# The first token group of a Mamba2 scan with a GELU network behind it: `a` in rows, B and C turned in blocks, another order of loads, y in the bank area

## The chip, the cores and the metric

The kernel runs on one core of one Trainium2 chip. The metric is the time of one execution on the device in microseconds; several executions are timed and the median is given. One further execution is taken with the hardware profiler, and every profile line below is from that one. PE is the matrix engine (PEld its weight loads), DVE the vector engine, ACT the scalar engine, POOL the general one, and SP the engine that here only issues DMAs.

## What is computed

A selective state space scan (Mamba2 SSD) over 4 batches of 8 heads, 768 positions, head dimension 32 and state dimension 16, and then a two-layer network with the quick GELU over the 3072 tokens. Cut to what matters:

```python
log_a = np.log(np.clip(a, 1e-06, 1.0))
for c in range(nc):                       # chunks along the sequence
    cum = np.cumsum(la, axis=-1)
    L = np.exp(cum[:, :, :, None] - cum[:, :, None, :]) * causal
    CB = np.einsum('bhin,bhjn->bhij', Cc, Bc)
    y_intra = np.einsum('bhij,bhjd->bhid', CB * L, xc)
    y_inter = np.einsum('bhin,bhnd->bhid', Cc, state) * decay_to_i[:, :, :, None]
    y[:, :, sl] = y_intra + y_inter
    state = decay_full[:, :, None, None] * state + np.sum(Bx, axis=2)
x = y.transpose(0, 2, 1, 3).reshape(3072, 256)
h = x @ w_in                              # 256 x 2048, given as float64
g = h * (1.0 / (1.0 + np.exp(-1.702 * h)))
out = (g @ w_out).astype(np.float32)      # 2048 x 256, given as float64
```

The two weight matrices come in as 64-bit floats and are made into 32-bit ones on the chip.

## The kernel before

**Tiling.** The 3072 tokens are six groups of 512 (`TG`). A group is two *pairs*, numbered p = 0 to 11; a pair is two blocks `k` of 128 positions, and each block has two chunks (`SIDES`) of 64. Groups 1 to 5 go through the same steps as group 0, but for groups 1 and later much of the work is laid between the matrix products of the group before it. Group 0 has nothing to hide behind. This document is about group 0 and the hand-over to what follows.

**A pair's scan.** `differ` puts differences of the cumulated logs of `a` into PSUM (after `mask` has put in the causal mask), `decay_exp` makes the decay matrix `L` of them. `turn_only` turns B and C with four transposes on PE and copies the results out of PSUM: `BT`, the per-head-masked `CT`, and plain C. `score` multiplies them into `cb`, `weigh` multiplies `L` by `cb` on DVE. `ends` scales B by the decay to the chunk's end, `gain` multiplies by x into the states' increments, `keep` (`part_of`, then `add_up`) turns these into states on DVE. `since_exp` and `since_start` scale C by the decay since the sequence's start. `finish` then makes y from two parts, `inter` (states) and `intra` (`L` and x), and ACT copies y to `yT`, or, for pair 0, to `early_y`.

**The first group's own form.** Rows of `a` come four times into 32 partitions each, 512 columns wide (`az0`), and are clipped, logged and scanned (L310 to L318) into `cum`. Pair 0's y lies in two PSUM banks, so `inter` is split into two halves around `intra`, tied by a POOL memset of `spare` (L738). Later pairs (`apart`) have y in the four-bank area `psa`.

**The network.** w_in comes in six pieces and w_out in four (`PIECES`; four small ones of 512 columns for hidden blocks 0 to 7, the rest with 1024). Piece i goes through `fields` (two DVE operations on the high words), `clamp` (two on ACT), `rounded` and `join` (one and two on DVE); `narrow(i)` is `rounded(i)`, `fields(i + 1)`, `join(i)`. `join` of some pieces also issues the load of a later one (`NEXT`). `half(j, t)` makes two hidden blocks for one pair (t = 0 for pair 0), `hidden(0, f)` one block for the whole group, and `project_all` the outputs. Before, blocks 0 to 3 are made in halves: `half(0, 0)` and `half(1, 0)` for pair 0, the second with four filling matmul instructions of ones, then `finish((1,))`, then `half(0, 1)` and `half(1, 1)`.

**What sets the order.** Every engine runs its instructions in the order in which the program text issues them (`in_order` adds that order as dependencies). PSUM has four banks in a ring (`bank`, tag `ff`) and one four-bank area (`area`, tag `cb`). The order of group 0 is written out by hand from L1043 to L1098, and what is laid into the hidden and project loops is listed by `at(...)` from L1106 on. All loads go through SP's queue in program order, but for two of `a`'s and C of pair 0 on ACT's:

```python
    rows_a(az0, (nc.sync, nc.scalar))
    ...
    load(0, nc.scalar)
    table(AF.Ln)
    fetch(0)
    load(1)
    for i in range(1, 4):
        fetch(i)
    rows_a(az, (nc.sync,))
```

Of the kernel before, what the change touches and what calls it, by code (L numbers as in the profile page):

```python
# [16 lines left out]
P = 128  # L17
# [18 lines left out]
def kernel(  # L36
# [71 lines left out]
    az0 = ssd.tile([P, CG, P], FP32, tag="CT", name="az0")  # L108
    cum = ffn.tile([P, 4 * TG // 2], FP32, tag="mg", name="cum", bufs=3)[:, :CG * P].rearrange(
        "p (c s) -> p c s", c=CG)  # L110
# [6 lines left out]
    def load_blocks(p):  # L117

        g, n = divmod(p, PG)
        b, c = divmod(2 * p, NC)  # L120
        for name, src in (("B", B), ("C", C)):
            if n == 0:
                blocks[name, g] = raw.tile([P, 2, PG * P], FP32, tag="z", name=f"z{name}{g}", bufs=2)
            for r in range(R):
                nc.sync.dma_start(
                    out=blocks[name, g][32 * r:32 * r + 32, :, n * P:(n + 1) * P],
                    in_=src[b, 2 * r:2 * r + 2, c * P:(c + 2) * P].rearrange(
                        "h (i f) n -> i h (f n)", i=32))

    def load(p, queue=nc.sync):  # L130
        rb[p] = raw.tile([P, 2, NH, N], FP32, tag="b", name=f"b{p}", bufs=3)
        if p < 2 * PG:
            rc[p] = raw.tile([P, 2, NH, N], FP32, tag="c", name=f"c{p}", bufs=3)
        else:
            load_blocks(p)
        rx[p] = raw.tile([P, 2, NH, D], FP32, tag="x", name=f"x{p}", bufs=3)
        for dst, src in ((rb, B), (rc, C), (rx, x)):
            for k in range(2 if p in dst else 0):
                b, c = divmod(2 * p + k, NC)
                sl = slice(c * P, (c + 1) * P)  # L140
                (queue if dst is rc else nc.sync).dma_start(out=dst[p][:, k], in_=src[b, :, sl, :].rearrange("h s d -> s h d"))  # L141
# [116 lines left out]
    rows_a(az0, (nc.sync, nc.scalar))  # L258
    early = const.tile([P, 1], FP32, name="early")
    spare = const.tile([P, 1], FP32, name="spare")  # L260
# [6 lines left out]
    load(0, nc.scalar)  # L267
    table(AF.Ln)
    fetch(0)
    load(1)  # L270
    for i in range(1, 4):
# [34 lines left out]
    carry = ssd.tile([P, NC, P], FP32, tag="first", name="carry", bufs=1)  # L306
    nc.vector.memset(carry[:, :CG], 1.0)
    nc.vector.memset(carry[:, :CG].rearrange(by_chunk, s=2)[:, :, :, 0], 0.0)

    nc.vector.tensor_scalar(out=az0, in0=az0, scalar1=1e-6, scalar2=1.0, op0=ALU.max,  # L310
                            op1=ALU.min)
    for k in range(2):
        nc.scalar.activation(cum[:, 2 * k:2 * k + 2], az0[:, 2 * k:2 * k + 2], AF.Ln)
    table(AF.Exp)
    for k in range(2):
        t = cum[:, 2 * k:2 * k + 2].rearrange("p c s -> p (c s)")

        nc.vector.tensor_tensor_scan(  # L318
            out=t, data0=carry[:, 2 * k:2 * k + 2].rearrange("p c s -> p (c s)"), data1=t,
            initial=0.0, op0=ALU.mult, op1=ALU.add)  # L320
# [12 lines left out]
    def pick_a(p):  # L333
# [4 lines left out]
        for q in range(Q):  # L338
# [3 lines left out]
    whose = const.tile([32, NH, N], FP32, name="whose")  # L342
    nc.gpsimd.memset(whose, 1.0)
    nc.gpsimd.affine_select(out=whose, in_=whose, pattern=[[-1, NH], [0, N]],
                            compare_op=ALU.is_equal, fill=0.0, base=0, channel_multiplier=1)


# [8 lines left out]
    idents = const.tile([P, 2 * NH, H], FP32, name="idents")  # L356
# [41 lines left out]
    def keep_busy(n):  # L398

        t = bank("busy")  # L400
        for i in range(n):
            nc.tensor.matmul(out=t, lhsT=ones, rhs=ones.unsqueeze(1).to_broadcast([P, 4, P]),
# [46 lines left out]
    def fan_rows(t, c0, c1):  # L449

        o = bank(f"rows{c0}")[:, :(c1 - c0) * P]
        nc.tensor.matmul(out=o, lhsT=whose.rearrange("p h n -> p (h n)"),
# [878 lines left out]
```

## Time and profile before

| what | value |
|---|---|
| median of three runs | 358.86 us (357.01, 358.86, 360.74) |
| the profiled execution | 359.47 us |
| its span | 357.4 us |
| granted TensorE clock, mean | 0.995 |
| busy PE / DVE / ACT / POOL | 349.4 / 251.6 / 148.7 / 10.5 us |
| first projection product (o) starts | 53.91 us |

The span is the time between the first and the last instruction of the program in the profile. Busy time is summed over each engine's instructions; a line such as `L212` is a line of the kernel's text. A timeline row has the start, the length, engine, line, operation, the tile written and the tiles read, the number of instructions merged into the row, and in brackets how long the engine was idle before it and what ended that. Rows of merged instructions may contain short gaps.

### The profile page before, as it was taken

What the parts mean: (1) busy time and instruction counts of PE and PEld (TensorE: products, weight loads), DVE (VectorE), ACT (ScalarE), POOL (GpSimd) and SP (SyncE); (2) the same over time, 40 slices, a digit from 0 to 9 for tenths busy, and PEclk for the clock granted to TensorE, in tenths of its full rate; (3) what the DMA queues carried; (4) which work ended last, traced back from release to release, by engine and by line L of the source; (5) the groups of instructions that cost most, each with busy time, mean ns of one, the idle gap of its engine ahead of it and who ended that gap; (6) DMA issues with size and microseconds to landing.
All of it is one profiled execution on the core that took longest, in us unless ns stands there. A gap on an engine that the chain in (4) does not pass through costs nothing.

```text
span 357.4 us, 9060 instructions
## 1 busy us (share of the span) xinstructions
PE 349.4 (98%) x3884; PEld 301.0 (84%) x3884; DVE 251.6 (70%) x480; ACT 148.7 (42%) x334; POOL 10.5 (3%) x36
## 2 busy tenths in 40 slices
PE   8979999999999999999999999999999999999996
PEld 3756448887679999889999889999989999989996
DVE  5777997999887999687588366588374344365363
ACT  5648837212353421753423454333454331453320
POOL 4200000100000100000000000000000000000000
PEclk9989999999999999999999999999999999999999
DMA  9897688316672000565006044000010000010001
GB/s 155 198 350 162 176 194 193 64 17 193 110 144 61 0 2 2 81 186 105 2 7 124 5 106 91 0 2 2 1 62 2 2 1 2 0 59 2 0 2 59
DMA packets 74527, 26.10 MB, mean 73 GB/s; under 512 B 60536, under 2 KB 67960, under 8 KB 74488
## 3 DMA queue, kind: packets, MB, share of 16 engines
q1 hardware_dynamic: 71896, 25.08, 30.0%
q10 hardware_dynamic: 2592, 0.46, 0.7%
q8 instruction: 30, 0.49, 0.6%
q14 instruction: 9, 0.07, 0.1%
HBM read 22.28 MB, written 3.24 MB: 71 GB/s over the span
## 4 chain that ended last, share of the span: by engine, by line
PE 89%; DVE 4%; SPq 2%; DMA 2%; ACT 1%; issue 1%
PE acc L956 35%; PE X L850 18%; PE Y L860 13%; PE o L892 8%; PE h L774 6%; PE y L728 2%; SPq L141 2%; PE y L705 2%; PE cb L597 2%; DMA bits<-in_moe_w_in_dram 1%; PE A L628 1%; PE h L792 1%; DVE p L206 1%; DMA az<-in_a_dram 1%; DVE w_in L212 1%
## 5 line engine op out<-in xcount | busy, mean ns | idle before, releaser
L956 PEld LDWEIGHTS acc<-mw,mg 128*128 128x128 f32 x480 | 67.1, 191 | 4.0
L956 PE MATMUL acc<-mw,mg 128*128 128x128 f32 x480 | 68.9, 275 | 0.0
L855 ACT ACTIVATE ac<-X 128x256 f32<-128x256 f32 x76 | 29.1, 382 | 83.5 <-PE X L850 83.0
L975 DVE TENSOR_TENSOR gT<-Y,ac 128x512 f32<-128x512 f32 x38 | 26.2, 690 | 41.3 <-PE Y L860 36.3
L827 ACT ACTIVATE gT<-gT 128x512 f32<-128x512 f32 (+1 forms) x76 | 39.3, 519 | 32.3 <-DVE gT L975 31.8
L956 PEld LDWEIGHTS acc<-w_out,gT 128*128 128x128 f32 x320 | 44.1, 191 | 2.6
L956 PE MATMUL acc<-w_out,gT 128*128 128x128 f32 x320 | 45.3, 275 | 0.0
L850 PE MATMUL X<-my,mi 128*128 128x256 f32 x152 | 45.2, 380 | 0.0
L975 DVE TENSOR_TENSOR gT<-Y,b 128x256 f32<-128x256 f32 x38 | 15.9, 420 | 35.0 <-PE Y L860 35.0
L892 PE MATMUL o<-w_out,gT 128*128 128x256 f32 x128 | 28.6, 381 | 0.0
L774 PE MATMUL h<-yT,w_in 128*128 128x512 f32 x64 | 28.3, 595 | 0.2 <-DVE w_in L212 0.2
L818 DVE TENSOR_TENSOR mg<-gT 128x512 f32<-128x512 f32 x40 | 27.2, 681 | 0.0
L892 PEld LDWEIGHTS o<-w_out,gT 128*128 128x128 f32 x128 | 23.9, 190 | 3.5 <-DVE w_out L212 0.2
L850 PEld LDWEIGHTS X<-my,mi 128*128 128x128 f32 x152 | 24.7, 191 | 1.3
L956 PEld LDWEIGHTS acc<-mw,gT 128*128 128x128 f32 x160 | 23.1, 191 | 1.8
L956 PE MATMUL acc<-mw,gT 128*128 128x128 f32 x160 | 24.3, 276 | 0.0
L774 PEld LDWEIGHTS h<-yT,w_in 128*128 128x128 f32 x64 | 11.9, 190 | 14.6 <-issue 12.7
L956 PE MATMUL acc<-w_out,mg 128*128 128x128 f32 x160 | 24.0, 275 | 0.0
L956 PEld LDWEIGHTS acc<-w_out,mg 128*128 128x128 f32 x160 | 22.8, 191 | 1.2
L855 ACT ACTIVATE b<-X 128x256 f32<-128x256 f32 x38 | 14.6, 383 | 21.4 <-PE X L850 20.9
L850 PE MATMUL X<-yT,w_in 128*128 128x256 f32 x76 | 23.3, 391 | 0.0
L860 PE MATMUL Y<-yT,mi 128*128 128x256 f32 x76 | 22.8, 381 | 0.3 <-DVE gT L975 0.3
(143 smaller groups left out, 510.2 us busy)
## 6 DMA issues: line engine op xcount, KB each, us to landing
a<-scratch SPq DMA_DIRECT2D x18, 256.0 KB
bits<-in_moe_w_out_dram SPq DMA_DIRECT2D x4, 1024.0 KB
x<-in_x_dram SPq DMA_DIRECT2D x24, 128.0 KB
out_dram<-c SPq DMA_DIRECT2D x9, 256.0 KB
bits<-in_moe_w_in_dram SPq DMA_DIRECT2D x4, 512.0 KB
bits<-in_moe_w_in_dram SPq DMA_DIRECT2D x2, 1024.0 KB
b<-in_B_dram SPq DMA_DIRECT2D x24, 64.0 KB
af<-in_a_dram SPq DMA_DIRECT2D x3, 384.0 KB
```

The lines of the kernel that those rows point to most:

```text
L141: (queue if dst is rc else nc.sync).dma_start(out=dst[p][:, k], in_=src[b, :, sl, :].rearrange("h s d -> s h d"))
L597: nc.tensor.matmul(out=s["cb"][side, r, k].rearrange("p (q i) -> p q i", q=Q), lhsT=BT[rows, k, side], rhs=CT[rows, k, :, side], start=Tru ...
L705: nc.tensor.matmul(out=y[i][to:to + Q * D, t, 2 * n + k], lhsT=old[rows], rhs=st[p]["CsT"][rows, k, SIDES[i]], start=begin(i, t, range(Q * ...
L774: nc.tensor.matmul(out=h, lhsT=w_in[:, k, f * P:(f + 1) * P], rhs=yT[g][:, k], start=(k == 0), stop=(k == NK - 1))
L818: nc.vector.tensor_tensor(out=t[:, 0:2], in0=B[:, :, 1], in1=B[:, 0], op=ALU.subtract)
L827: nc.scalar.activation(o, i, AF.Silu, scale=GELU_SCALE)
L850: nc.tensor.matmul(out=s["X"], lhsT=lhsT, rhs=rhs, start=i == "1", stop=i == "4", skip_group_check=True)
L855: nc.scalar.activation(copy, s["X"], AF.Copy)
L860: nc.tensor.matmul(out=o, lhsT=lhsT, rhs=rhs, start=s.pop("new", False), stop=i != "5", skip_group_check=True)
L892: nc.tensor.matmul(out=o[k // 2][:, k % 2], lhsT=gT[g, f // 2][:, f % 2, k * P:(k + 1) * P], rhs=w_out[:, f], start=(f == 0 and k % 2 == 0 ...
L956: nc.tensor.matmul(out=o[k] if type(o) is list else o[:, cols], lhsT=h[:, cols], rhs=w, start=(j == 0 and (i, k) in begins), stop=(j == NF ...
L975: nc.vector.tensor_tensor(out=o, in0=v, in1=w, op=ALU.add)
```

## The change

It concerns group 0, and the places of group 1's work that are listed beside it.

- `az0` and `cum` hold pair 0's and pair 1's 256 positions of batch 0 in different rows, 256 columns instead of 512; one log, one scan. `differ` reads row sets 0 and 2 (`ROW`), and `whose` gets four row sets. `since_exp` is done per pair.
- B and C of pair 0 are also loaded in 512-byte runs (`load_blocks`, now two DMAs for each of B and C instead of four, with `queues`), and turned by DVE (`turn_first`) instead of PE; `mask_first` makes `CT`. Pair 0's B is still loaded in the other form for `ends`.
- The loads come in another order: blocks, piece 0, b0, x0, then C and B of pair 1, piece 1, x of pair 1, pieces 2 and 3.
- Pair 0's decay matrix is made by one exponential over the area; pair 1's masks and differences come directly after pair 0's.
- `finish` has y in the area for all pairs; for pairs 0 and 1 `intra` goes ahead of `inter`. The `spare` memset and the ties are gone.
- Only blocks 0 and 1 are made in halves, with pair 1's score and decay between the two blocks of `half(0, 0)`. The filling matmuls in `half` are gone, and those of `keep_busy` are four times as many of a quarter of the width. The explicit load of the Silu table is gone.
- `narrow`, `clamp` and group 1's steps have other places in the loops of group 0.

```diff
-    az0 = ssd.tile([P, CG, P], FP32, tag="CT", name="az0")
+    az0 = const.tile([P, 2, P], FP32, name="az0")
+    cum = const.tile([P, 2, P], FP32, name="cum")
...
+            for h in range(2):
+                queue.dma_start(
+                    out=blocks[name, g][:, h, n * P:(n + 1) * P],
+                    in_=src[b, h::2, c * P:(c + 2) * P].rearrange("r (i f) n -> r i (f n)", i=32))
...
-    rows_a(az0, (nc.sync, nc.scalar))
+    for r in range(R):
+        (nc.sync, nc.scalar)[r % 2].dma_start(
+            out=az0[32 * r:32 * r + 32].rearrange("p k s -> p (k s)"),
+            in_=a[:2, :, :TG].rearrange("b h (c s) -> c (b h) s", c=PG))
...
-    load(0, nc.scalar)
+    load_blocks(0, (nc.scalar, nc.sync))
     table(AF.Ln)
     fetch(0)
-    load(1)
-    for i in range(1, 4):
+    load(0, "b")
+    load(0, "x")
+    load(1, "cb")
+    fetch(1)
+    load(1, "x")
+    for i in range(2, 4):
         fetch(i)
...
+    def turn_first(name):
+        t = ssd.tile([P, TG], FP32, tag=f"{name}t", name=f"{name}t0", bufs=1)[:, :2 * P]
+        nc.vector.transpose(
+            out=t.rearrange("p (i f) -> p f i", i=32),
+            in_=blocks.pop((name, 0))[:, :, :P].rearrange("p h (f n) -> p f h n", n=N))
...
+    def mask_first():
+        s = st[0]
+        s["CT"] = ssd.tile([P, 2, Q, P], FP32, tag="CT", name="CT0")
+        nc.vector.tensor_tensor(
+            out=s["CT"], in0=s["tp"].unsqueeze(2).to_broadcast([P, 2, Q, P]),
+            in1=part.unsqueeze(1).unsqueeze(3).to_broadcast([P, 2, Q, P]), op=ALU.mult)
...
-        for i in range(n):
-            nc.tensor.matmul(out=t, lhsT=ones, rhs=ones.unsqueeze(1).to_broadcast([P, 4, P]),
+        for i in range(4 * n):
+            nc.tensor.matmul(out=t[:, :P], lhsT=ones, rhs=ones,
...
+        early = pairs[0] < PG
+        y = area(f"y{pairs[0]}")[:, :, :len(pairs) * 2 * H].rearrange(
+            "p (s t) (k i) -> p s t k i", s=2, i=H)
...
+        for part in (intra, inter) if early else (inter, intra):
+            for n, p in enumerate(pairs):
+                part(n, p)
```

The order of group 0 after the change, from the masks on:

```python
    masked(1, range(3))
    turn_first("C")
    turn_first("B")
    mask_first()
    differ_of(0, range(R))
    decay_exp(0, None, ab0[:, :, :2 * Q * H])
    masked(1, range(3, R))
    differ_of(1, range(R))
    fields(0)
    rounded(0)
    fold_ident(1)          # the second half of the tile idents; the first stands ahead of the log
    score((0,), ab0)
    exps(1, range(R))
    since_exp(0)
    clamp(0)
    ends(0, 0, nc.gpsimd)
    ends(0, 1, nc.gpsimd)
    weigh(0)
    gain((0,))
    since_start(0, nc.gpsimd)
    keep(0)
    finish((0,))
    turn_only(1)
    join(0)
    ends(1, 0)
    ends(1, 1)
    fields(1)
    rounded(1)
    clamp(1)
    half(0, 0, second)     # second: score((1,)), since_exp(1), since_start(1, nc.gpsimd)
    gain((1,))
    weigh(1)
    keep(1, range(3))
    finish((1,))
    join(1)
    load(PG)
    spread_rows(1)
    fields(2)
    clamp(2)
    add_up(1, (3,))
```

And the places in the loops of group 0:

```diff
-    for i, k in ((2, 1), (3, 3), (4, 4), (5, 6)):
-        at(in_hidden[0], k, lambda i=i: narrow(i), lambda i=i: i < 5 and clamp(i + 1))
...
+    for i, k, c in ((2, 1, 1), (3, 2, 2), (4, 4, 4), (5, 6, 6), (6, 9, 12), (7, 12, 15)):
+        at(in_hidden[0], k, lambda i=i: narrow(i))
+        at(in_hidden[0], c, lambda i=i: clamp(i + 1))
...
-    at(in_project[0], 9, lambda: narrow(9))
-    at(in_project[0], 11, lambda: finish(pairs))
-    at(in_project[0], 14, lambda: mix_in(1), lambda: mix_y(1), lambda: mix_in(2),
-       lambda: mix_in(3), lambda: turn_blocks(2))
+    at(in_project[0], 13, lambda: finish(pairs))
+    at(in_project[0], 14, lambda: mix_in(1), lambda: mix_in(2), lambda: mix_in(3),
+       lambda: turn_blocks(2), lambda: mix_y(1), lambda: decay(n))
...
-        if f >= 4:
+        if f >= 2:
             hidden(0, f)
-        elif f % 2:
-            half(f // 2, 1, f == 1)
+        elif f == 1:
+            half(0, 1)
```

## Prediction

> **What bounds the kernel now.** I read the page first, then the chain that ended last, then the timeline of the first 60 us, then busy time by stretches. The page:
>
> ```profile
> span 357.4 us, 9060 instructions
> PE 349.4 (98%) x3884; PEld 301.0 (84%) x3884; DVE 251.6 (70%) x480; ACT 148.7 (42%) x334; POOL 10.5 (3%) x36
> ```
>
> PE is called busy for 98%, and that share hides a start in which other engines set the pace. The chain, pieces in order of time (start, us, what):
>
> ```profile
> 12.34 4.82 DMA bits<-in_moe_w_in_dram
> ...
> 21.43 3.68 PE h L792 x8
> ...
> 26.71 0.66 ACT yT L753 x2
> ...
> 38.22 3.67 PE h L774 x8
> ...
> 43.25 10.50 PE h L774 x24
> 54.19 3.46 PE o L892 x16
> ...
> 86.96 6.87 PE h L774 x16
> ```
>
> From 43 us on the chain is almost PE alone. Before that it goes through the landing of weight piece 1 (17.16), hidden products and the copy of the second pair's y (over at 27.37). So a change to the first group is worth what it takes from the moment PE's dense run begins, if the weights keep up. The timeline shows why that moment is late:
>
> ```profile
> 16.60 1.99 PE L792 MATMUL h<-y,w_in 128*128 128x256 f32 x8
> 17.18 0.62 DVE L179 TENSOR_SCALAR p<-bits 128x512 uint32<-128x512 uint32 x1 [1.23 <-DMA bits<-in_moe_w_in_dram]
> 21.43 3.68 PE L792 MATMUL h<-y,w_in 128*128 128x256 f32 x8 [1.97 <-DVE S L671]
> 26.71 0.66 ACT L753 ACTIVATE yT<-y 128x256 f32<-128x256 f32 x2 [0.97 <-PE y L705]
> 28.76 0.69 DVE L206 SCALAR_TENSOR_TENSOR p<-bits,p 128x512 uint32<-128x512 uint32 x1 [3.56 <-ACT p L191]
> 53.91 3.32 PEld L892 LDWEIGHTS o<-w_out,gT 128*128 128x128 f32 x16
> ```
>
> Two lines matter most. half(1,0) stands ahead of finish((1,)) on PE and takes 3.68 us where eight instructions of the same kind take 1.99 at 16.60. And DVE idles 3.56 us at 28.76: clamp(2) on ACT is queued behind the copies of y1. The stretches show the clock:
>
> ```profile
> 19.00:20.00 1.00, 0.46 (x3) 0.06 (x1) 0.94 (x2) 0.98 (x2) 0.00 (x0) 1.00 0.93 206
> 20.00:21.00 1.00, 0.00 (x0) 0.00 (x0) 0.97 (x4) 0.99 (x3) 0.00 (x0) 1.00 1.03 258
> 22.00:23.00 1.00, 1.00 (x4) 0.82 (x3) 1.00 (x2) 0.00 (x0) 0.00 (x0) 0.50 1.00 377
> ```
>
> (stretch, length, then busy us of PE, PEld, DVE, ACT, POOL, granted clock, DMA share, GB/s.) PE is idle for some 2 us and is then granted half its clock.
>
> **The sum's frame.** Let T be when y1 stands in yT: 27.37 now. From T to the first o product (53.91) are 26.5 us. I work out T after the change, then the run from T to the projection, then what is given back later.
>
> **Up to the decay of pair 0: nothing.** az0 and cum have half the columns, so one Ln and one scan of 256 replace two of each (0.36 and 0.72 each). But the old code already lets differ(0) start after the first half: Ln at 4.62, scan 5.07, PE 5.99. The Ln table is ready at 4.47 whatever the layout, and fold_ident(0) (128x512; the 128x1024 row is 1.21, so 0.6) now stands ahead of the clip. Seven masks instead of six: 0.14 more. differ(0) starts at 6.0 as now. The half-size loads of a are hidden behind the same table load; if they landed 1 us later, T would move by 1. keep_busy has the same columns in four times as many matmuls. No row has them at the start. The 128-column products of L956 come at 0.11 us each (8 in 0.89) against a weight load of 0.19, so loads hide and it stays at 3.6 us; if every cold load (0.25) stood bare, 16 x 0.25 = 4.0 us more, of which 2.7 reach differ(0). I take the nearer row, 0.
>
> **Pair 0.** One exp of 128x1024 instead of four (1.21 together): 1.15 by ACT's 128x1024 row L190, so it ends at 8.55 (now 8.62). On DVE the transposes of C and B replace the copy from PSUM (0.42): a 128x512 STREAM_TRANSPOSE is 1.10 here, a plain 128x256 operation 0.42; I take 0.6 each. With the mask (0.68), fields (0.8), rounded (0.7 to 1.2) and fold_ident(1) (0.6) DVE is free at 10.2, and weigh(0) (1.21) ends at 11.4, now 12.44. PE's score (0.70) and gain (0.48) lie before that. The transposes need z blocks at 5.8: 0.26 MB in 512-byte runs, between 0.8 us (the weights' 340 GB/s) and 2.2 us (120 GB/s in 3 to 4 us, the 64-byte rows), from 2.5 us on: hidden either way. keep(0) takes 0.47 + 0.93, to 12.8. The spare memset and its ties between the two halves of inter go. Because intra now goes ahead of inter and y lies in the area, 64 products run under keep(0); only inter (0.45) and the copies (0.66) are left: y0 stands at 14.05, now 16.17. since_exp(0), clamp(0) (0.72 + 0.72, done 11.95) and POOL's larger mask `whose` (0.53 now, up to 2.1, needed at 9.3) are covered. join(0) ends at 14.2 (now 15.96).
>
> **Loads.** SP's order becomes a, B blocks, piece 0, b0, x0, c1, b1, piece 1, x1; ACT's queue issues four as now (a, then C blocks). Ahead of piece 1 leave x1 (0.26 MB at 112 GB/s, the mean of 10 to 14 us: 2.3 us), b0 and c0 (2.2) and half of a (0.13 MB at 340 GB/s: 0.4); the blocks come in (0.8 to 2.2) and b0 behind piece 0 (0.13 MB at 120 GB/s down to 78, the mean of 9 to 11 us: 1.1 to 1.7). Piece 1 lands between 14.2 and 16.2 instead of 17.16; with 1.1 and 1.3, 14.7. For x0: a 0.4, blocks 1.1, piece 0 1.6, b0 1.3, itself 1.6 (160 GB/s) from 2.0 on give 8.0; the same sum for piece 0 now gives 8.2 where fields(0) got it at 9.3, so x0 lands near 9.1 and is needed at 9.9. Beyond that slack each us is a us of T. x1 lands near 17, needed at 17.4. Pieces 2 to 5 have about the same bytes ahead of them as now. The later block loads are half as many issues of twice the size, off the chain: nothing.
>
> **Pair 1.** ACT copies pair 1's turned tiles (0.38 + 0.83 + 0.39) behind y0, to 15.65, then clamp(1) to 17.1, since_exp(1) to 17.5, table load (1.28) and the Silu of half(0,0) to 19.4. DVE: ends(1) to 14.7, fields(1) 15.5, rounded(1) 16.2, weigh(1) 17.4, part_of 18.4, three additions (0.9) 19.35. inter ends at 19.85 and the copies at 20.55. **T = 20.6.** half(1,0), its fill and join(1) no longer stand ahead of it.
>
> **From T to the projection.** PE: half(0,1) 1.72 (8 x 0.215), hidden(0,2) to (0,15) 14 x 1.717 (four instructions of 0.43) = 24.0, the fan 1.4: 27.2. DVE: join(1) 20.75, fields(2) and the last addition 21.85, then 2.9 us for a small piece (0.69 + 0.83 + 1.38) and 4.95 for a large one (1.22 + 1.30 + 2.45). join(2) is done at 24.7 (needed 24.0 + 1.72), join(3) 28.1 (29.2), join(4) 33.0 (32.6: waits 0.4), join(5) 38.7 (42). clamp(6) now stands ahead of a Silu that frees a bank: 0.6 of wait at hidden(0,10). So 28.3 us: the projection begins at 48.9, 5.0 earlier.
>
> **After that.** narrow(6) to narrow(9) end at 47.5, 52.5, 57.9, 67.6 against needs of 49, 56.5, 64, 73: held. One thing comes back: decay(4) moves ahead of the ob copies and needs the spread rows, which SP issues at 79.85 behind x of pair 5, itself waiting for the pair 2 and 3 finish. DVE may stand 0 to 1.5 us for it; PE feels part, 0.5. **Gain 4.5.** The profiled execution is 359.47 us (span 357.4 and 2.1 around it): 354.97. The median shown, 358.86, lies 0.61 below that execution, so 354.4.
>
> [...] The fills in half are gone, and PE has gaps of about 1 us between 13 and 20. The row: after 1.97 us of idle the clock fell to 0.50 for about 3.4 us. [...] By the row a gap of 2 us costs 1.7 us, half of 3.4; my gaps stay below that, so I take 0 and keep 1.7 for the range.
>
> **Rivals.**
> 1. *Later T, smaller gain.* Piece 1 at 16.2 (1.5), x0 at 11 (1.1), or one half-clock stretch (1.7); one or two of them give 355.5 to 357.6. For: DMA is at or over 1.0 share for most of 3 to 28 us, with SP issues of up to 2.84 us. Against: fewer 64-byte rows ahead.
> 2. *DVE becomes the bound.* DVE is busy 4.96, 4.88 and 4.97 of 5 us at 30 to 45, and the sum leaves margins of 1 us at join(2) and join(3). If DVE's operations beside POOL run as rounded(0) did (1.17 against 0.69), some 3 to 4 us of the gain goes: 357.5 to 358.5. Against: the DVE idle at 28.76 is what is being used up.
> 3. *Slower: x0 starves the first pair.* gain(0), keep(0), y0 and all after them wait for x0, which is now behind 512 KB of weights and b0 on one queue. It decides when x0 lands 6.8 us after its need, past 16.7; at 20 the time is 362. For: x1, behind two small-row pairs, lands that late now. Against: the sum above has x0 through by 9.1, and b0 and c0 leave the space ahead of it.
> 4. *The layout does not do what it says*, the start gains nothing and T stays: 358.9.
>
> **How the numbers follow.** Forecast 0.56 (351.5 to 355.5); rival 1 0.2; rival 2 0.1, rival 4 0.05; slower 0.09. A measurement of this kernel tells about 1% (3.6 us) from no change: faster by over 1% is below 355.27, which the forecast and a little of rival 1 give, 0.6; slower is above 362.4, 0.08; between, 0.32. The range goes from 351.0 (half of the margins unneeded, no give-back) to 359.5, which takes in rivals 1, 2 and 4.
>
> **What will show it.** y1's copies near 19.9 instead of 26.71; piece 1's fields(1) near 14.7 without a DMA wait; the first o product near 49; granted clock 1.00 from 20 to 30. The forecast is wrong if PE's h products wait for DVE w_in more than 2 us in all, if gain(0) starts after 11, or if the decay of pair 4 leaves PE idle before 95.

## The result and the profile after

The changed kernel is slower: 369.45 us median of four runs (366.62 to 370.82), 2.9% more than the kernel before on the same chip (ratio 1.029, interval 1.021 to 1.037). Medians here are of all executions of a run, while ratios are against the kernel before on the same chip and leave out executions in the chip's slower state, so what an edit is worth is read from the ratios (1% is 3.6 us). Its profiled execution took 369.09 us. The page of after:

```profile
span 367.4 us, 9007 instructions
PE 352.2 (96%) x3880; PEld 302.6 (82%) x3880; DVE 250.7 (68%) x479; ACT 148.0 (40%) x329; POOL 11.2 (3%) x34
```

Expected were 4.5 us less, so two stretches have to be explained: the start, which gained almost nothing, and the stretch from 54 to 100 us, where the rest was lost. The chain that ended last in after (start, us, what) shows both at once, because it now runs through transfers where it ran through PE before:

```profile
3.37 8.08 DMA zC<-in_C_dram
...
58.87 5.82 DMA bits<-in_moe_w_out_dram
...
89.55 5.32 DMA a<-scratch
94.89 2.30 DVE L L381
98.36 5.40 PE h L778 x8
```

**The start.** The timeline of after (start, us, engine, line, operation, tiles, and in brackets the idle time before it and what ended that):

```profile
6.39 0.29 DVE L324 TENSOR_SCALAR az<-az 128x256 f32<-128x256 f32 x1 [2.50 <-DMA az<-in_a_dram]
6.90 5.45 SPq L139 DMA_DIRECT2D x<-in_x_dram  x2
11.55 0.64 DVE L567 STREAM_TRANSPOSE Ct<-zC 128x256 f32<-128x256 f32 x1 [3.63 <-DMA zC<-in_C_dram]
13.32 0.88 PE L621 MATMUL ab<-CT,Bt 32*64 32x128 f32 x32 [2.56 <-DVE CT L590]
25.79 0.66 ACT L757 ACTIVATE yT<-y 128x256 f32<-128x256 f32 x2 [1.26 <-PE y L725]
54.36 3.62 PE L895 MATMUL o<-w_out,gT 128*128 128x256 f32 x16
```

`a` was clipped at 4.16 before and is clipped at 6.39 now, from half the bytes. The blocks of C are turned only at 11.55, after DVE stood 3.63 us for them. y1 is copied at 25.79 (26.71 before, 19.9 forecast), and the first output product stands at 54.36 (54.02 before). Busy time by stretches, first after, then before (stretch, length, busy us of PE, PEld, DVE, ACT, POOL, granted clock, DMA share, GB/s):

```profile
3.00:6.40 3.40, 3.40 (x17) 2.63 (x15) 0.85 (x4) 1.49 (x2) 2.78 (x6) 1.00 0.45 131
9.00:10.00 1.00, 1.00 (x45) 0.62 (x37) 0.00 (x0) 0.67 (x1) 0.00 (x0) 1.00 0.32 66
10.00:11.00 1.00, 0.76 (x24) 0.54 (x16) 0.00 (x0) 0.58 (x2) 0.00 (x0) 1.00 0.22 57
14.00:16.00 2.00, 1.96 (x42) 0.93 (x34) 2.00 (x3) 0.61 (x2) 0.15 (x1) 0.50 1.08 103
```

```profile
3.00:6.40 3.40, 2.85 (x38) 1.39 (x39) 2.25 (x5) 3.23 (x5) 2.11 (x6) 1.00 1.32 151
```

The loads are awaited while the DMA share is 0.22 to 0.45, against 1.32 in before from 3 to 6.4 us. So the transfers are late though by this share most of the DMA engines stand idle (a rough reading, as the view's share can exceed 1). Behind PE's gap from 10.8 to 13.3 the clock falls to 0.50.

**From 54 us on.** DVE in after waits for the last two weight pieces and for the rows of pair 4:

```profile
57.22 0.69 DVE L177 TENSOR_SCALAR p<-bits 128x1024 uint32<-128x1024 uint32 x1 [4.07 <-DMA bits<-in_moe_w_out_dram]
64.78 0.69 DVE L177 TENSOR_SCALAR p<-bits 128x1024 uint32<-128x1024 uint32 x1 [1.91 <-DMA bits<-in_moe_w_out_dram]
94.89 2.29 DVE L381 TENSOR_TENSOR_SCAN L<-a,idents 128x1024 f32<-128x1024 f32 x1 [4.38 <-DMA a<-scratch]
98.36 5.40 PE L778 MATMUL h<-yT,w_in 128*128 128x512 f32 x8 [2.09 <-DVE ob L901]
```

The same piece in before, piece 8 at 53.05, had no wait in front of it:

```profile
53.05 0.69 DVE L179 TENSOR_SCALAR p<-bits 128x1024 uint32<-128x1024 uint32 x1
```

The gain of the pairs after these (PE `A`) starts at 93.76 in before and at 103.69 in after. At 54 us the kernels were level, so all 10 us are lost between 54 and 104. Busy time in stretches of 5 us gives an account of them; the last line of each is the sum from 54 to 104, first after with the two stretches at a lower clock, then before:

```profile
74.00:79.00 5.00, 4.42 (x123) 3.69 (x124) 4.84 (x9) 0.00 (x0) 0.74 (x1) 0.66 0.06 8
...
99.00:104.00 5.00, 5.00 (x41) 1.94 (x40) 3.27 (x5) 0.80 (x2) 0.00 (x0) 0.66 0.59 161
sum 50.00, PE 44.51 PEld 33.65 DVE 37.20 ACT 11.87 POOL 1.06; mean PE 4.45 PEld 3.36 DVE 3.72 ACT 1.19 POOL 0.11
```

```profile
sum 50.00, PE 49.66 PEld 39.39 DVE 44.57 ACT 18.68 POOL 1.06; mean PE 4.97 PEld 3.94 DVE 4.46 ACT 1.87 POOL 0.11
```

PE stands 5.2 us more (49.66 less 44.51), and two stretches at a clock of 0.66, which before hasn't, lose 0.34 x 5 = 1.7 us each. That makes 8.6 of the 10 us. The waits on PE's side are for operations that were queued behind the waiting DVE (engine, line, for whom, total, times, longest):

```profile
PE A L652 <- DVE CsT L607: 2.2, 1, 2.2
PE h L778 <- DVE ob L901: 2.1, 1, 2.1
```

### The profile page after: what moved, and what is told of

It reads as the page before. It is cut to its first block, busy times and chain, and to the rows that moved or that the text cites. A ratio compares the mean times of both kernels' runs of the same rounds, so it can differ in the third digit from the quotient of the medians.

```text
span 367.4 us, 9007 instructions
## 1 busy us (share of the span) xinstructions
PE 352.2 (96%) x3880; PEld 302.6 (82%) x3880; DVE 250.7 (68%) x479; ACT 148.0 (40%) x329; POOL 11.2 (3%) x34
## 4 chain that ended last, share of the span: by engine, by line
PE 82%; DVE 9%; DMA 5%; issue 1%; ACTq 1%; ACT 0%; SPq 0%; POOL 0%; DVEq 0%; POOLq 0%
PE acc L959 34%; PE X L853 18%; PE Y L863 13%; PE h L778 8%; DMA zC<-in_C_dram 2%; PE y L737 2%; PE y L725 2%; DMA bits<-in_moe_w_out_dram 2%; DMA a<-scratch 1%; PE cb L621 1%; PE h L795 1%; DVE L L381 1%; DVE mi L815 1%; PE A L652 1%; PE o L895 1%; DVE L L632 1%
## 5 line engine op out<-in xcount | busy, mean ns | idle before, releaser
L778 PE MATMUL h<-yT,w_in 128*128 128x512 f32 x72 | 33.5, 621 | 2.1 <-DVE ob L901 2.1
L778 PEld LDWEIGHTS h<-yT,w_in 128*128 128x128 f32 x72 | 14.1, 198 | 19.4 <-issue 15.7
L821 DVE TENSOR_TENSOR mg<-gT 128x512 f32<-128x512 f32 x40 | 27.2, 681 | 0.0
L381 DVE TENSOR_TENSOR_SCAN L<-a,idents 128x1024 f32<-128x1024 f32 x9 | 20.6, 2285 | 4.4 <-DMA a<-scratch 4.4
```

Of the source, the lines that this page charges most:

```text
L381: nc.vector.tensor_tensor_scan(out=L, data0=ra[p].rearrange("p k e -> p (k e)"), data1=idents.rearrange("p h i -> p (h i)"), initial=0.0, ...
L778: nc.tensor.matmul(out=h, lhsT=w_in[:, k, f * P:(f + 1) * P], rhs=yT[g][:, k], start=(k == 0), stop=(k == NK - 1))
L821: nc.vector.tensor_tensor(out=t[:, 0:2], in0=B[:, :, 1], in1=B[:, 0], op=ALU.subtract)
```

## Two theories for the loss

*Engines.* The new sources of `az0` (`c (b h) s`, c = 2) and of the blocks (`r i (f n)`, r = 4) have a slowest dimension of 2 and 4. The theory (K in the expectations) supposes that their loads are moved by only 2 and 4 of the 16 DMA engines. What speaks for it is the DMA share in after: 0.12 from 3 to 4 us, while `a` is on its way, and 0.22 to 0.32 at 9 to 11 us, while C's blocks are, near 2 of 16 = 0.125 and 4 of 16 = 0.25. So the two numbers are an estimate from the share; the views don't show which engines ran. Against it stood the view that short runs and the order of the loads alone make them late.

*Places.* The new places of `narrow` and of `decay(4)` let DVE meet transfers that haven't landed; the queue behind DVE then stands. Against it stood the view that a late start alone makes these pieces late.

## The experiments on the two theories

**Rows of a with a slowest dimension of 16.** After, with the slowest dimension of the source 16 instead of 2; `pick0` and `whose0` follow the other order of rows.

```diff
-            in_=a[:2, :, :TG].rearrange("b h (c s) -> c (b h) s", c=PG))
+            in_=a[:2, :, :TG].rearrange("b h (c s) -> (b h) c s", c=PG))
...
-    ROW = {0: 0, 1: 2}
+    ROW = {0: 0, 1: 1}
```

> The changed kernel, with a's rows for the first group put down in the order (head, block) instead of (block, head), so that the source's slowest dimension has 16 steps instead of 2; the selecting tiles follow. Same bytes, runs of 1 KB and number of DMAs. Theory K (a DMA whose source has a slow dimension of 2 or 4 runs on 2 or 4 of the 16 DMA engines): the clip of a starts near 4.3 us instead of 6.39; the blocks still crowd four engines, so the transposes start at 9 to 11 instead of 11.55 and the whole gains 0 to 2 us (367 to 369.5). [...] Rival S (short runs and the new order of loads are what is slow): the clip stays at 6.4 and the time at 369.5.

Measured: 364.09 us, ratio 1.014 (1.010 to 1.018). That is 1.5% or some 5.4 us below after, more than the 0 to 2 us expected. The clip comes at 5.74 without a DMA wait, the first transpose still waits 1.81 us for C's blocks and stands at 9.48, y1 at 23.34, the first output product at 51.91. The rest of the gain lies behind that: piece 8 is awaited 1.70 us instead of 4.07, decay(4) 3.00 instead of 4.38. So one rearranged source gives back about 5 us.

**Blocks with a slowest dimension of 32.** After, with four DMAs each for B and C as before the change, slowest dimension 32.

```diff
-            for h in range(2):
+            for r in range(R):
-                    in_=src[b, h::2, c * P:(c + 2) * P].rearrange("r (i f) n -> r i (f n)", i=32))
+                    in_=src[b, 2 * r:2 * r + 2, c * P:(c + 2) * P].rearrange(
+                        "h (i f) n -> i h (f n)", i=32))
```

> The changed kernel, with the block loads of all groups issued as four DMAs per tensor and pair, 32 partitions each, whose slowest dimension has 32 steps, instead of two with 4 steps. Same bytes and runs of 512 bytes, twice as many issues. Theory K: the blocks are in by 7 to 8 us (behind a's rows on two engines), the transposes start at 7.9 to 8.5 instead of 11.55, y1's copies at 22 to 24 instead of 25.79; the whole gains 2 to 5 us (364.5 to 367.5). Rival S: twice the issues make the start later, 370 or more.

Measured: 365.83 us, ratio 1.015 (1.006 to 1.024), 1.4% or some 5.1 us below after. Its profiled execution took 372.44 us, the longest of its four, so no times of it are read; in it no wait stands in front of the transposes.

**Both.**

> Both edits of the two runs before this one in the list. Theory K: clip near 4.3, first transpose near 6.5, y1's copies near 20 to 21.5, as the prediction's schedule had them; the weights of w_out are then fetched some 5 us earlier and the projection does not wait for them; 355 to 360 us. Rival S: no gain over the changed kernel, 369 to 371. Rival P (most of the loss arises in the projection, by the order of group 1's steps there, whatever the start does): 363 to 367.

Measured: 366.01 us, ratio 1.015 (1.006 to 1.024). The clip runs at 5.75 without a DMA wait (DVE is held by `minus`, which waits 1.61 us for POOL's `pick0`), the transposes at 7.59, and y1 at 21.61, near the forecast's 19.9. And still the end is no better than with either of the two. The DVE rows show waits for three transfers; the first is new, those for piece 9 and for the rows of pair 4 were there in after as well (1.91 and 4.38):

```profile
28.47 0.69 DVE L178 TENSOR_SCALAR p<-bits 128x1024 uint32<-128x1024 uint32 x1 [1.91 <-DMA bits<-in_moe_w_in_dram]
60.33 0.69 DVE L178 TENSOR_SCALAR p<-bits 128x1024 uint32<-128x1024 uint32 x1 [2.25 <-DMA bits<-in_moe_w_out_dram]
88.98 2.29 DVE L393 TENSOR_TENSOR_SCAN L<-a,idents 128x1024 f32<-128x1024 f32 x1 [2.92 <-DMA a<-scratch]
```

So the two fixes together give what each gives alone, 1.4%, though the intervals nearly allow their sum. What is left of the loss lies behind the start, which the theory of the places takes up.

**decay(4) back behind the ob copies.**

```diff
-       lambda: turn_blocks(2), lambda: mix_y(1), lambda: decay(n))
+       lambda: turn_blocks(2), lambda: mix_y(1))
-    at(after, "H0", lambda: decay(n + 1), lambda: since_start(n),
+    at(after, "H0", lambda: decay(n), lambda: decay(n + 1), lambda: since_start(n),
```

> The changed kernel, with the decay of pair 4 put back behind the first two hidden blocks of group 1, where it stood before the change. Theory K: the 4.4 us that VectorE waits for the spread rows at 90 us goes off the chain, the ob copies come 4 to 6 us earlier and the hidden blocks of group 1 with them; but the decay itself is late by then, so 1 to 4 us are gained (365.5 to 368.5). Rival P (the loss arises here): 6 us or more, 363 or less. If the order does not matter: 369.5.

Measured: 365.34 us, ratio 1.016 (1.010 to 1.023), 1.3% or some 4.7 us below after (the intervals just touch). The row of decay(4) waits 0.53 instead of 4.38 us:

```profile
93.91 2.29 DVE L381 TENSOR_TENSOR_SCAN L<-a,idents 128x1024 f32<-128x1024 f32 x1 [0.53 <-DMA a<-scratch]
```

**Only the places of narrow and clamp 6 to 9 as before.**

```diff
-    for i, k, c in ((2, 1, 1), (3, 2, 2), (4, 4, 4), (5, 6, 6), (6, 9, 12), (7, 12, 15)):
+    for i, k, c in ((2, 1, 1), (3, 2, 2), (4, 4, 4), (5, 6, 9), (6, 11, 15)):
...
-    at(in_project[0], 0, lambda: turn(PG), lambda: narrow(8))
-    at(in_project[0], 1, lambda: clamp(9))
+    at(in_project[0], 0, lambda: turn_only(PG), lambda: narrow(7), lambda: since_start(PG))
...
-    at(in_project[0], 5, lambda: narrow(9))
+    at(in_project[0], 4, lambda: narrow(8))
+    at(in_project[0], 6, lambda: clamp(9))
...
+    at(in_project[0], 9, lambda: narrow(9))
```

> The changed kernel, with only the places of clamp(6) to clamp(9) and narrow(6) to narrow(9) back where they stood before; gain, finish and the decay of pair 4 stay at the changed places. Theory W: the waits for pieces 8 and 9 (4.07 and 1.91 us) go, the decay of pair 4 still holds up the ob copies; 363 to 366. If the places of narrow carry all of the loss: 359 to 361. Rival L: 368 or more.

Measured: 365.24 us, ratio 1.020 (1.014 to 1.026), 0.9% or some 3.2 us below after, which the two intervals don't tell from nothing. The rows say more: piece 9 isn't awaited at all, while piece 8 is awaited as long as in after, and decay(4) still is:

```profile
57.68 0.69 DVE L177 TENSOR_SCALAR p<-bits 128x1024 uint32<-128x1024 uint32 x1 [4.14 <-DMA bits<-in_moe_w_out_dram]
92.08 2.29 DVE L381 TENSOR_TENSOR_SCAN L<-a,idents 128x1024 f32<-128x1024 f32 x1 [3.43 <-DMA a<-scratch]
```

So the places of `narrow` aren't what makes piece 8 late. SP's rows, first of after, then of before, show its load issued 5.6 us later, behind the eight stores of `a` to `scratch`, which take SP 8.66 us instead of 3.31:

```profile
38.90 8.66 SPq L1124 DMA_DIRECT2D scratch<-az  x8
49.36 0.59 SPq L165 DMA_DIRECT2D bits<-in_moe_w_out_dram  x1
```

```profile
38.92 3.31 SPq L1110 DMA_DIRECT2D scratch<-az  x8
43.73 0.59 SPq L167 DMA_DIRECT2D bits<-in_moe_w_out_dram  x1
```

No run changed what stands ahead of this load, so that is read from the rows and not tested.

**All places and decay(4) as before, the start as after.** This joins the two edits above and also puts narrow 2 to 5 with their clamps, `pick_a`, the gain and the finish of group 1 where they stood.

> [...] Theory W (the changed kernel reached the projection as early as before, 54.5 us, and lost its ten us there: fields(8) and fields(9), pulled ahead of group 1's decay, wait in VectorE's order for weight pieces whose buffers are only just freed, and the decay of pair 4 waits for its spread rows ahead of the ob copies): no DMA wait above 1 us at fields(8) and fields(9), group 1's first hidden block at 87 to 89 and 358.5 to 361 us. Rival L (the loss comes from loads running late since the start, wherever the steps stand): fields(8) still waits 3 to 4 us, 364 or more.

Measured: 361.34 us, ratio 1.008 (1.004 to 1.012), 2.1% or some 7.5 us below after; the two parts, 4.7 and 3.2, make about that. Piece 9 and decay(4) aren't awaited any more; piece 8 still is, for 2.96 us where less than 1 was expected, and the time is just above the expected 358.5 to 361. y1 stands at 25.51 and the first output product at 54.41, as in after: the places cost nothing before 54 us and some 7 us behind it.

**Both sources as in these runs and all places as before.**

> Both parts at once: a's rows with 16 steps and blocks with 32 steps in the slowest dimension (as in the run that had both), and the places in the loops of group 0 as before. Theories K and W together: the projection starts at 51.5 to 52.5 (the start gains 1.5 to 2 us, no more, since weight piece 4 is issued 3 us later than before) and runs 33 us as before; 356 to 358.5. If the start's gain is lost again: 359 or more.

Measured: 358.08 us, ratio 0.999 (0.996 to 1.002): what was lost against before is back. By the ratios the two sources give 1.4% (5.1 us) with the new places and 0.9% (3.3 us) with the old ones, the places alone 2.1% (7.5 us), all together 3.0% (10.8 us). What is left of the change's start is y1 at 22.76 and the gain of the later pairs at 91.16 (93.76 in the profile of before), and of that the time shows nothing beyond its interval.

**The same form of source in the kernel before, where it is off the path.** Only the block loads of the later groups, with slowest dimension 4.

```diff
-            for r in range(R):
+            for h in range(2):
-                    in_=src[b, 2 * r:2 * r + 2, c * P:(c + 2) * P].rearrange(
-                        "h (i f) n -> i h (f n)", i=32))
+                    in_=src[b, h::2, c * P:(c + 2) * P].rearrange("r (i f) n -> r i (f n)", i=32))
```

> The kernel before, with only the block loads of the later groups in the changed form (two DMAs per tensor and pair with a slowest dimension of 4, instead of four DMAs of 32 steps). Theory K: each runs on four engines and takes longer, but these loads have tens of us in hand; within 1 us of the kernel before (357.6 to 359.6). If they cost something throughout: 360 or more.

Measured: 357.57 us, ratio 1.000 (0.996 to 1.003). Off the path it costs nothing. This run gives a warning as well: its start has no edit, and yet its y1 stands at 24.61, its first output product at 51.94 and the gain of the later pairs at 91.67, 2 us ahead of the profile of before; its profiled execution took 357.50 us against 359.47. The clock goes with it: here PE waits 1.09 us ahead of half(1,0) and the clock stays at 1.00 from 18 to 28 us (its mean over the profiled execution is 1.000), in the profile of before it waits 1.97 us and the clock is 0.50 from 22 to 24. So the forecast started from an execution with such a stretch, and by these rows about 2 us of what it saw to gain aren't there in one without it. Against the rows of this run the kernel with both causes undone is only 0.5 us ahead (91.16 against 91.67).

**The same form on the path.** The kernel before, and only the source of `az0`'s four loads split with 2 outermost.

```diff
-    rows_a(az0, (nc.sync, nc.scalar))
+    for r in range(R):
+        (nc.sync, nc.scalar)[r % 2].dma_start(
+            out=az0[32 * r:32 * r + 32].rearrange("p c s -> p (c s)"),
+            in_=a.rearrange("b h s -> (b h) s").rearrange("(m u) s -> u m s", u=2)[:, :, :TG])
```

> The kernel before; only the source of az0's four loads is written with the rows split in (32/2) x 2 and the 2 outermost, so that each DMA walks 2 long strides outside 16 short ones; bytes and run length (2048) are the same. The rows of a then stand in another order, so the heads get each other's decay and the output is not the reference's; the instructions and their shapes are the same. If the slowest dimension of the source sets how many DMA engines move it, the four loads of 64 KB run on 2 engines: the DMA share from 2 to 6 us falls toward 0.12 to 0.25, the clip moves from 4.16 to 7 to 10 us, the chain behind it moves with it for what pair 0's 64-byte rows do not hide, and the median is 360 to 364. Rival: run length and bytes set it, as the order of strides is nothing to them: the clip stays within 0.5 us of 4.16 and the median at 358 to 359.

Measured: 368.20 us, ratio 1.027 (1.023 to 1.031). Bytes, run length, queue and instructions are those of before; only the order of the strides differs. The timeline, and four stretches of it, with one of before behind them:

```profile
9.09 0.43 DVE L313 TENSOR_SCALAR az<-az 128x512 f32<-128x512 f32 x1 [5.53 <-DMA az<-in_a_dram]
10.75 1.16 PE L495 MATMUL ab<-cum,pick 32*64 32x128 f32 x32 [4.48 <-DVE cum L321]
```

```profile
2.00:3.00 1.00, 1.00 (x2) 0.34 (x1) 0.37 (x3) 0.00 (x0) 0.84 (x4) 1.00 0.06 10
8.00:9.00 1.00, 0.00 (x0) 0.00 (x0) 0.00 (x0) 0.00 (x0) 0.00 (x0) 1.00 0.16 32
10.00:12.00 2.00, 1.25 (x36) 0.92 (x36) 2.00 (x4) 1.76 (x3) 0.00 (x0) 0.50 0.89 170
24.00:26.00 2.00, 2.00 (x93) 1.59 (x95) 1.93 (x5) 1.26 (x5) 0.10 (x1) 0.50 0.96 280
```

```profile
2.00:3.00 1.00, 1.00 (x2) 0.34 (x1) 0.37 (x3) 0.02 (x1) 0.85 (x4) 1.00 0.81 237
```

The clip moves from 4.16 to 9.09, as the engines theory said. The DMA share is 0.06 at the start of the load and 0.16 just ahead of the clip (2 engines of 16 would be 0.125); between 4 and 8 us other loads run beside it and it is higher. The end moves by 9.6 us, more than the 1 to 5 expected. The last two stretches of this run show what that left out: during PE's wait of 4.48 us the clock falls to 0.50, and it stays there in all stretches up to 30 us; y1 is copied at 35.03 instead of 26.71. What the clock alone makes of the 9.6 us wasn't measured apart. The view that short runs and order alone make `a` late falls here: runs and order are unchanged.

## The experiments on what was left of the gain

With both causes undone the kernel is level with before, and the forecast's 4.5 us are still missing.

**Weight pieces 4 and 5 ahead of the loads of az** (the four `rows_a(az, ...)` moved behind them), on the kernel with both sources mended and old places.

> The same kernel with both sources at 16 and all places as before; only pieces 4 and 5 are issued ahead of the four loads of az. If the loop after y1 is bound by when the weight pieces land, piece 4's fields start about 2 us earlier, the DVE wait for its bits (1.9 us in the run with both sources at 16) goes, and the median falls by 0.5 to 1.5 us to 356.6 to 357.6. If it is bound by y1 and PE, it stays at 358.1 within 0.5, and az landing later may cost since_fanned nothing, as it is needed only in the second half of the hidden loop.

Measured: 359.62 us, ratio 1.003 (1.000 to 1.005). No gain, and not 358.1 within 0.5 either, though the 0.4% to the same kernel without this edit lie within the intervals. Piece 4 isn't awaited any more (0.37 us without the edit), y1 stands at 22.77 and the first output product at 51.34, but piece 8 is awaited 4.16 us instead of 1.33. SP issues it at 46.85 instead of 45.15, again behind the stores of `a`, which take SP 7.95 us instead of 6.93. The expectation of a gain was wrong.

**An earlier start** on the same kernel: Ln table ahead of the issues of C's blocks, `minus` after the scan, the second fold of the identity behind `weigh(1)`, and the order of pieces of the experiment just told.

```diff
-    load_blocks(0, (nc.scalar, nc.sync))
     table(AF.Ln)
+    load_blocks(0, (nc.scalar, nc.sync))
```

> The kernel with both sources at 16 and all places as before, whose y1 copies begin at 22.76 and whose median is 358.08, with its start mended further: the Ln table is loaded ahead of the issues of C's blocks (in that run ACT idled to 4.23 and the clip ran at 5.73 behind DVE's `minus`, which waited 1.61 us for POOL's pick), `minus` is made after the scan, the second fold of the identity stands between weigh(1) and keep(1), and pieces 4 and 5 are issued ahead of the loads of az. If the order of the small operations at the start still costs what that run shows, the clip begins near 4.3, pair 0's gain and y0 come about 1.2 us earlier, y1's copies begin at 20.5 to 21.8, the first o product near 50, and the median is 355 to 357, which is the best of all these kernels and below the kernel before by about 0.6%. Rival: from y1 on the loop is bound by the weights (piece 4's and fields(8)'s bits), so that an earlier y1 changes the end by less than 0.5 us: 357.6 to 358.6.

Measured: 359.34 us, ratio 1.004 (1.001 to 1.006). The clip runs at 4.29 and y0 is copied at 14.37, both as hoped, but y1 comes later than without the edit, at 24.61. The timeline shows what it waited for:

```profile
12.12 0.32 PE L663 MATMUL A<-x,Be 64*32 64x64 f32 x13 [1.20 <-DMA x<-in_x_dram]
12.54 0.62 SPq L166 DMA_DIRECT2D bits<-in_moe_w_in_dram  x1
16.80 0.47 PE L560 MATMUL tp<-ident,b 128*128 128x128 f32 x1 [2.09 <-DMA b<-in_B_dram]
17.94 0.43 DVE L178 TENSOR_SCALAR p<-bits 128x512 uint32<-128x512 uint32 x1 [0.87 <-DMA bits<-in_moe_w_in_dram]
```

x of pair 0, b of pair 1 and piece 1 are all late; the clock falls again at 13 to 14 us, behind the wait of 1.20 for x, and is 0.50 in all of 14 to 18 us, through the wait of 2.09 (see below).

**Long rows.** The last question: do the small runs of b, c and x set these three landings? Same kernel, with the ten loads of pairs 0 and 1 taken from as many bytes that lie together.

```diff
+                if p < 2:
+                    nc.sync.dma_start(
+                        out=dst[p][:, k].rearrange("s h d -> s (h d)"),
+                        in_=src[b].rearrange("h s d -> (h s d)")[c * P * NH * e:(c + 1) * P * NH * e]
+                        .rearrange("(s f) -> s f", s=P))
```

> The kernel with the early start (both sources at 16, places as before, Ln table first; clip at 4.29, y0 copies at 14.37, but pair 1's b awaited 2.09 us at 16.80, x of pair 0 awaited 1.20 us at 12.12, piece 1 awaited 0.87 us at 17.94, y1 copies at 24.61, median 359.34). Changed here: b, c and x of pairs 0 and 1 are read as the same number of bytes that lie together in memory, so that each partition gets one run of 512 bytes (b, c) or 1024 bytes (x) instead of eight of 64 or 128; the values then stand at other positions and the output is not the reference's; instructions, order and queue are the same. If it is the small runs of the two pairs that set when x0, b1 and piece 1 land (the loads late anyway), these three waits go, piece 1's fields begin by 15.0, y1's copies begin at 20.5 to 22, the first o product is near 50 and the median is 355 to 357.5. Rival: the waits come from how SP issues and the queue takes up descriptors in order, whatever their runs: b1 still awaited by over 1 us, y1's copies after 23.5, and the median at 358.5 to 359.5. Third: y1 comes early and the end does not, because the w_out pieces are late (fields(8) awaited 2.34 us there): y1's copies before 22, the median still over 358.

Measured: 354.85 us (354.66 to 355.53), ratio 0.990 (0.987 to 0.994), 1.0% or some 3.5 us below before and 1.3% below the same kernel with the small runs (1.004). The timeline shows piece 1 issued at 8.81 instead of 12.54, and no DMA wait left at x, at b or at piece 1:

```profile
8.81 0.43 SPq L172 DMA_DIRECT2D bits<-in_moe_w_in_dram  x1
10.45 0.47 PE L669 MATMUL A<-x,Be 64*32 64x64 f32 x32
13.33 0.44 PE L566 MATMUL tp<-ident,b 128*128 128x128 f32 x2
15.39 0.41 DVE L184 TENSOR_SCALAR p<-bits 128x512 uint32<-128x512 uint32 x1
20.65 0.66 ACT L774 ACTIVATE yT<-y 128x256 f32<-128x256 f32 x2 [1.16 <-PE y L742]
49.22 3.62 PE L912 MATMUL o<-w_out,gT 128*128 128x256 f32 x16
```

The stretch from 14 to 18 us with the small runs (first) and with the long ones:

```profile
14.00:18.00 4.00, 1.91 (x14) 1.41 (x13) 2.34 (x6) 0.92 (x3) 0.78 (x1) 0.50 0.88 202
```

```profile
14.00:18.00 4.00, 3.20 (x42) 2.10 (x42) 3.97 (x8) 3.52 (x9) 1.27 (x2) 1.00 0.99 339
```

The clock stays at 1.00, and y1 is 4.0 us earlier. (The 339 GB/s instead of 202 aren't for the same transfers: with the long runs the queue is at later weight pieces by then.) That is the start that the forecast had in mind, with loads that the real data layout doesn't give: 5 loads of two DMAs, each 1024 runs of 64 or 128 bytes.

## Why the prediction was wrong, step by step

1. **"The half-size loads of a are hidden", and the blocks "hidden either way".** This step failed. The bounds (0.8 to 2.2 us for the blocks, 0.4 for half of `a`) were byte rates of loads with a slowest dimension of 16 or more. `az0` was there 2.2 us later than before with half the bytes (the same form on before, 262 KB, has a piece of 6.81 us in its chain: 38 GB/s); C's blocks took 8.08 us in the chain. differ(0) began at 7.91 (6.0 forecast), the scores at 13.32, y0 at 18.44 (13.4). The prediction had noted the half-sized loads and the fewer, larger issues, and didn't look at what became the slowest dimension. With both sources mended, y0 stood at 14.54 to 15.68 in three runs.

2. **"x0 lands near 9.1", "piece 1 14.7".** This step was mis-sized apart from the first. It summed bytes by GB/s along SP's queue. With both sources mended (the early start) x0 was used at 12.12, straight from its landing, and piece 1 at 17.94, because SP issued it at 12.54, practically where it did before (12.34). The issue of two DMAs of small runs took SP 1.1 to 2.8 us there, against 0.4 to 0.6 for a weight piece; from the issue of b0 to that of piece 1 it was 7.6 us, and 3.9 with long runs. Taking such loads from ahead of piece 1 and putting others there left its issue where it was. With the small runs gone, piece 1's fields ran at 15.39 (forecast 14.7), y0's copies at 13.46 (13.4), y1's at 20.65 (19.9) and the first output product at 49.22 (48.9). So the sums of the engines' work, up to T and from T to the projection, were right to about 1 us (27.2, 0.4 and 0.6 make 28.2 and not 28.3, which changes nothing); it was the loads under them that failed. (That kernel also has both sources mended, the places of before, and the table and two small operations in another order.)

3. **"narrow(6) to narrow(9) ... held".** This step failed. The sum counted DVE's time for a piece against the need of PE and left out when pieces 8 and 9 land. `narrow(7)` was done at 60.9 and `narrow(8)` at 68.5 (52.5 and 57.9 forecast). Piece 8 was issued at 49.36 (43.73 before) and awaited 4.07 us; as it is awaited with the old places too (4.14 and 2.96 us), the rows put this wait down to SP's queue and not to the places. The earlier `narrow(8)` then waited 1.91 us for piece 9 in front of pair 3's decay and rows on DVE, and PE stood 2.2 us at `A` for what was queued behind. With the places of `narrow` undone the wait for piece 9 was gone; the time fell by 3.2 us, which is within its intervals, and by 7.5 with all places undone, which isn't.

4. **decay(4), "DVE may stand 0 to 1.5 us; PE feels part, 0.5".** The mechanism was named and the size was off: DVE stood 4.38 us, the ob copies behind it came late, and PE stood 2.09 us for them at 98.36. Undone: some 4.7 us. The spread rows were read as due after their issue of 79.85, in the old order; in after SP issued them at 88.86, behind x of pair 5.

5. **The clock.** The prediction kept 1.7 us for one half-clock stretch and took none. In after the clock was 0.50 from 14 to 20 us, and the two stretches at 0.66 behind the waits of steps 3 and 4 cost 3.4 us by the account above. The mean clocks of the two profiles, 0.981 over 367.4 us and 0.995 over 357.4, put the time that PE's clock was held back at some 7.0 us in after and 1.8 in before (an estimate of the most it can have cost). As the falls come behind the waits, their share wasn't measured alone; nor was the removal of the fills in `half` tried alone.

Of the signs that the prediction named for being wrong, one came as written: gain(0) began at 15.28 (limit 11). Another came late: decay(4) left PE idle, but at 96.3 to 98.4 and not before 95. Waits of the hidden products for w_in didn't come in after.

What held: the transposes took 0.64 and 0.62 us (0.6 forecast), the exponential of 128x1024 1.02 (1.15), `keep_busy` with four times as many matmuls 3.79 us (3.6), and the later block loads cost nothing (ratio 1.000). Of the rivals the third had the right side for a wrong reason: a load did starve the first pair, but C's blocks and not x0, and the larger part of the loss was none of the rivals: it lay in the projection.

What stays open: by the ratios the source of `a` alone gave 5.4 us, that of the blocks 5.1, and both together 5.1. The intervals of up to 0.9% either way nearly allow the sum of the two, so whether they truly don't add up isn't shown; the three transfers awaited in the run with both weren't taken away one by one there. Nor was it tried to move the stores of `a` and the loads that stand on SP's queue ahead of piece 8. No version was found that has the right output and beats before; 358.08 us is level with it.

## What to carry to other kernels

When a load is rewritten, write down its source's dimensions from the outside in before anything else: here a slowest dimension of 2 in place of 32 brought the same bytes 4.9 us later, and an awaited load with a low DMA share (0.16 there, 0.22 to 0.32 in after) was the sign of it in the profile. Small runs are to be costed by the time that their issue holds the queue for all that stands behind (1.1 to 2.8 us for two DMAs here), not by bytes. And when work is moved forward in an engine's order, the question is not only whether that engine has the time, but when the transfer it reads is issued and by whom: a wait moved ahead of other work costs that work too.

## What the runs showed of the hardware

- The order of strides in a source alone changed when the same 262 KB were there: used at 4.16 us with the slowest dimension 32, at 9.09 us with 2. In after, with 2 and 4, the DMA share was 0.12 from 3 to 4 us, while `a` was on its way, and 0.22 to 0.32 from 9 to 11, while the blocks were. In the run with 2 alone it was 0.16 in the last stretch ahead of the clip. 2 of 16 would be 0.125 and 4 of 16 0.25; how many engines ran isn't in these views.
- The granted clock fell to 0.50 within about 2 us after a PE wait of only 1.20 us (the early start) and behind one of 1.97 us (before), while it stayed at 1.00 behind one of 1.09 us (the run with the later blocks alone) and behind one of 1.43 us (after, at 7.91, with 1.00 in every stretch from 6 to 13 us). So these rows show no length of wait that decides it. Around one of 4.48 us it was down for some 20 us (0.50 in all stretches from 10 to 30 us), though PE is shown busy for nearly all of the stretches after the wait.
- The same bytes in runs of 512 and 1024 bytes instead of 64 and 128: the issue of two such loads took SP 0.9 to 1.8 us instead of 1.1 to 2.8, and piece 1 behind them was issued at 8.81 instead of 12.54. With the small runs 85 GB/s were moved at a DMA share of 0.80 from 10 to 14 us; with the long ones it was 300 at 0.92, but by then partly for weight pieces.
